# New orders for the attention stage of a parallel transformer block, and a weight split moved to GpSimd

## Chip, cores and metric

The kernel runs on one core of a Trainium2 chip. The metric is the device time in microseconds (us) of one execution. TensorE (PE, its weight loads PEld), VectorE (DVE), ScalarE (ACT), GpSimd (POOL) and the DMA queue of SyncE (SP) each work through their own instructions in program order; semaphores make one wait for another.

## What is computed

A row of 448 values for each of 2048 tokens is normalised, goes through multi-query attention (16 heads of 28, one shared key and value head) and, normalised again, through a channel MLP (448 to 1792 to 448, GELU). The sum of input, attention and MLP is the output, all in float32:

```python
def _A_ref(x, wq, wk, wv, wo):          # S=2048, D=448, H=16, Dh=28
    q = (x @ wq).reshape(B, S, H, Dh).transpose(0, 2, 1, 3)
    k, v = x @ wk, x @ wv
    scores = einsum("bhqd,bkd->bhqk", q, k) * (Dh ** -0.5)
    o = einsum("bhqk,bkd->bhqd", softmax(scores), v)
    return o.transpose(0, 2, 1, 3).reshape(B, S, H * Dh) @ wo
xn = layernorm(x)
return x + _A_ref(xn, wq, wk, wv, wo) + _B_ref(xn, w1, b1, w2, b2)   # _B_ref: layernorm, GELU MLP
```

## The kernel before, in words

The first part (to about 349 us of the span) normalises, makes queries, keys and values and runs the MLP. It is not changed. Its last steps already compute the scores of the first two key tiles of attention.

Attention is 16 units, `units`: four chunks of 512 query tokens times four groups of four heads. A unit meets 16 key tiles of 128 tokens. All of TensorE's results go to the eight banks of PSUM (each 128 partitions by 512 floats), which are handed out in a ring: `bank_number` takes the next one modulo 8 (L606), so that a user waits for whoever read the bank eight turns ago. The pieces of work are:

- `scores` (L612), one key tile: four banks, one for each head; 12 matmuls of 32x512 (L618), three terms of the split float32 product, the four heads side by side on four row strips of the array. Then ScalarE takes exponentials from the banks to a tile `p` in SBUF (L625). A digit after the `s` in the order says which neighbouring banks share an instruction: bit j joins bank j with bank j+1 (s5 = 0-1 and 2-3, s6 = 0 and 1-2-3, s2 = 0, 1-2, 3, s4 = 0, 1, 2-3, s1 = 0-1, 2, 3, s0 = four apart). Banks 7 and 0 are not neighbours, so a join across the ring's end falls away.
- `pv` (L735), the weighted sum of 1, 2 or 3 key tiles (P1, P2, P3): one bank; eight matmul instructions a key tile (L739), four heads on four column strips, in plain float32 and so in two passes. VectorE then adds the bank to a running sum `oc` (L731 the first, L733 the others) and so frees it. The weighted sums run two key tiles behind the scores.
- `m`, `find_max` (L540): one matmul against the first key tile (L523) for a bound on the next unit's scores, then four VectorE steps and a DMA (L524 to L531) that put the bound into that unit's queries. These queries come by four DMAs, issued at the start of the unit before (`load_unit`, L533, L538).
- `Q`, `out_tile` (L703): the output product of one tile of 128 tokens of the chunk before, 12 matmuls (L701) with the split output weights `woh`, `wol`, a VectorE add to the loaded row and a DMA out. `T` does the same ahead of time for the last chunk, `E` is the last weighted sum and the end of the kernel.
- After a unit's last weighted sum VectorE normalises (L714 to L722) in two parts, put in between the adds, and GpSimd makes the low half of the split result (L723).

Nothing but a table sets the order: `ORDERS` (L34) has one string for units 0 to 3, one for 4 to 14, one for 15. The loop at L836 goes through its words and calls these pieces, and each engine gets its instructions in that order. After the third word of unit 0 the loop also calls `split_out` (L681), which splits the output weights `wor` into a rounded high half and the rest. `wor` comes by four DMAs issued when attention begins (L678).

Of the kernel before, what the change touches and what calls it, by code (L numbers as in the profile page):

```python
# [14 lines left out]
ALU = mybir.AluOpType  # L15
# [15 lines left out]
MLP_ORDER = 1, 2, 3, 0  # L31
HD = D // 2
WEIGHTS = 7
ORDERS = ("s5 P1 s6 s6 P2 s6 s5 P2 s4 s1 m P2 s6 P1 s6 s5 P2 s6 s6 P2 s6 s5 P2 s6 s4 P2",  # L34
          "s5 P1 s6 s6 P2 s6 s5 P2 s6 s6 P2 s6 s5 P2 s2 s2 P2 s2 m Q s2 s6 P3 s6 s4 P2",
          "s5 P1 s6 s6 P2 s6 s5 P2 s6 s6 P2 s6 s5 P2 s2 s2 P2 s2 m Q s2 s6 P2 T T T E3")
FIRST_BANK = 0
LIMITS = 0.25, 2.0 ** 40

# [2 lines left out]
def block_kernel(ctx, tc, x, wq, wk, wv, wo, w1, b1, w2, b2, out):  # L42
    nc = tc.nc
    pe, act, dve, pool = nc.tensor, nc.scalar, nc.vector, nc.gpsimd
    ctx.enter_context(tc.manual_schedule())

    def f(t):
        return t.bitcast(F32)
# [418 lines left out]
    for c in range(NCH):  # L467
        if c + 1 < NCH:
            center, turn = norm_parts(c + 1, False)
        for i in range(4):  # L470
# [24 lines left out]
            if i in ((1, 3), (1, 2), (1, 3), (0, 2))[c]:  # L495
                n = 2 * c + (i - 1 if c == 1 else i // 2 if c == 3 else i // 3)
# [36 lines left out]
    def load_unit(u):  # L533
        c, g = units[u]
        qs = qss[u] = qst[u % 2]
        for j in range(4):
            rs = slice(DH * (4 * g + j), DH * (4 * g + j + 1))
            nc.sync.dma_start(f(qs[32 * j:32 * j + DH, :, :]), qd[rs, :, c * CW:(c + 1) * CW])  # L538
# [73 lines left out]
    def scores(u, kt, joined):  # L612
        at = [bank_number() for j in range(4)]
        keys = slice(kt * P, (kt + 1) * P)
        for n, (i, h) in enumerate(((0, 0), (0, 1), (1, 0))):
            for j in range(4):
                rs = slice(32 * j, 32 * j + 32)
                pe.matmul(bank(at[j]), ks[rs, i, keys], qss[u][rs, h, :], start=(n == 0), stop=(n == 2))  # L618
        p = early.pop(0) if early else att.tile([P, 4, CW], F32, name=f"p{next(turn_p) % WEIGHTS}", bufs=1)
        j = 0  # L620
        while j < 4:
            n = 1
            while j + n < 4 and joined >> (j + n - 1) & 1 and at[j + n] == at[j] + n:
                n += 1
            act.activation(p[:, j:j + n, :], banks[:, at[j]:at[j] + n, :], AF.Exp, scale=SCALE)  # L625
            j += n
        ps[u, kt] = p
# [43 lines left out]
    def weights_tile():  # L671
        t = xl_p.tile([P, 4, CW], F32R, name="xl").rearrange("p b n -> p (b n)")
        return t[:, 0:NG * D].rearrange("p (g d) -> p g d", g=NG)

    wor = f(weights_tile())
# [3 lines left out]
    woh, wol = weights_tile(), weights_tile()  # L679

    def split_out():  # L681
        dve.tensor_copy(woh, wor)
        dve.tensor_sub(wol, wor, f(woh))


    sums = keep.tile([P, NU, CW // 32], F32, name="sums")
# [3 lines left out]
    def load_rows_of(c):  # L690
        for k in range(CT):
            rows[c, k] = att.tile([P, D], F32, name="row", bufs=2 * CT)
            nc.sync.dma_start(rows[c, k], ad[:, CT * c + k, :])
# [55 lines left out]
    def last_burst(n, flag):  # L749
        u = NU - 1  # L750
        c, g = units[u]
        oc = pos.pop(u)
        tr, rb = (att.tile([P, CW], F32, name=name) for name in ("tr2", "tr"))
        rc = att.tile([P, CW // 32], F32, name="rc")
        halves = [(slice(256 * i, 256 * i + 256), slice(8 * i, 8 * i + 8)) for i in range(2)]
        sides = []
        for h, r in halves:
            po = score_bank()[:, 0:256]
            for k in range(NT - n, NT):
                for j in range(4):  # L760
                    pe.matmul(po[32 * j:32 * j + 32, :], vs[:, k, :], ps[u, k][:, j, h],
                              start=(k == NT - n), stop=(k == NT - 1))
            sides.append(po)
        ahead(CT - 1)
        for i, (h, r) in enumerate(halves):
            dve.tensor_add(oc[:, h], oc[:, h], sides[i])
            dve.transpose(tr[:, h], oc[:, h])
            if i == 1:
                copy = flag(blocks(tr)[:, :, 0])
            dve.reciprocal(rc[:, r], blocks(tr[:, h])[:, :, 0])  # L770
            dve.transpose(blocks(rb[:, h]), rc[:, r, None].to_broadcast([P, 8, 32]))
            dve.tensor_mul(oc[:, h], oc[:, h], rb[:, h])
            if i == 1:
                copy()
            for k in (2 * i, 2 * i + 1):
                pe.matmul(outs[k], oc[:, k * P:(k + 1) * P], wor[:, g, :], start=False, stop=True)  # L776
        for k in range(CT):
            a = rows[c, k]
            if k == 1:
                act.activation(tr[:, 0:D], outs[k], AF.Copy)  # L780
                pool.tensor_add(a, a, tr[:, 0:D])
            else:
                dve.tensor_add(a, a, outs[k])
            (nc.scalar if k % 2 else nc.sync).dma_start(ov[:, CT * c + k, :], a)
# [6 lines left out]
    def weighted(count):  # L791
        n = done[0]
        done[0] += count
        u, kt = divmod(n, NT)
        pv(u, kt, count)
        n += count - 1
        if n % NT == NT - 1:
            norm = norm_jobs(u, pos.pop(u))
            soon(n + 1, lambda: next(norm))
            soon(n + 3, lambda: next(norm))  # L800
        for m in sorted(at):
            if m <= n:
                for job in at.pop(m):
                    job()

    def token(kind, u):
        if kind == "m" and u + 1 < NU:
            find_max(u + 1)
        elif kind == "m":
            extremes(sums.rearrange("p u e -> p (u e)").bitcast(I32), worst)  # L810
        elif kind == "Q":
            c, k = units[u]
            out_tile(c - 1, k, range(NG))
        elif kind == "T":
            ahead(len(outs))
# [20 lines left out]
    for u in range(NU):  # L836
        if u + 1 < NU:
            load_unit(u + 1)
        if units[u][1] == 0 and u:
            load_rows_of(units[u][0] - 1)  # L840
        if u == NU - 2:
            load_rows_of(NCH - 1)
        for n, word in enumerate(ORDERS[(u >= NG) + (u == NU - 1)].split()):
            kind, times = word[0], int(word[1:] or 1)
            if kind == "s" and todo:
                scores(*todo.pop(0), times)
            elif kind == "P":
                weighted(times)
            elif kind == "E":
                last_burst(times, flag)  # L850
            else:
                token(kind, u)
            if (u, n) == (0, 2):
                split_out()
    outside = nc.values_load(count)
    with tc.If(outside > 0, preferred_fallthrough_block=True, label="outside"):
# [45 lines left out]
```

## Time and profile before

| | us |
|---|---|
| median of 3 runs (lowest, highest) | 894.08 (893.58, 894.96) |
| the profiled execution's own time | 893.52 |
| its span, from first to last instruction | 891.7 |
| TensorE busy in the span | 875.2 |
| ScalarE busy in the span | 650.1 |
| VectorE busy in the span | 360.7 |
| GpSimd busy in the span | 155.3 |
| attention after its first stretch, 366.70 to 877.60 | 510.90 |
| of that ScalarE busy | 474.35 |

A row of the timeline has the start, the time to the end of the last instruction, the engine, the line, the operation, what is written from what is read, shapes and count; in brackets the engine's idle time before it and what ended that. Matmuls overlap in the array, so the distance from one row's start to the next one's start, and not the row's length, is what a burst costs. In a row of groups the numbers behind the bar are busy us in total, mean ns of one, and idle us before them with what ended it.

### The profile page before, as it was taken

To read this page: it belongs to the slowest core of one execution; us is meant where nothing else is said; L and a number is where in the kernel's file an instruction comes from. 1 tells how busy PE (TensorE), PEld (TensorE's weight loads), DVE (VectorE), ACT (ScalarE), POOL (GpSimd) and SP (SyncE) were. 2 spreads that over 40 slices of the span, in tenths; PEclk is the share of its full clock that TensorE was granted. 3 is DMA by queue.
4 is the path that set the end of the run, shared out by engine and by line. 5 is a ranking of instruction groups with operands and counts; after the bars stand their busy time and mean duration, and the time that the engine had idled before them with its cause. 6 is when DMAs were issued, how large, how long until landed. Compare 5 with 4: busy or idle time off the path is not lost.

```text
span 891.7 us, 16976 instructions
## 1 busy us (share of the span) xinstructions
PE 875.2 (98%) x6997; PEld 529.5 (59%) x6997; DVE 360.7 (40%) x654; ACT 650.1 (73%) x890; POOL 155.3 (17%) x149
## 2 busy tenths in 40 slices
PE   9999999999999999899999999999999999999997
PEld 8877888888888886333434444444444444444444
DVE  7865454335345353342343234233233233333323
ACT  5765443333443436799999898898898899899891
POOL 7443243242234332000000000000000000000000
PEclk9999999999999999999999999999999999999999
DMA  9792112002001103000002101102101102102001
GB/s 301 215 288 81 42 63 83 1 1 83 21 21 51 44 11 91 9 22 22 9 16 64 33 1 33 33 2 74 32 1 33 33 1 74 33 1 73 12 1 54
DMA packets 28957, 46.02 MB, mean 52 GB/s; under 512 B 4542, under 2 KB 20492, under 8 KB 28876
## 3 DMA queue, kind: packets, MB, share of 16 engines
q1 hardware_dynamic: 27468, 44.32, 16.1%
q8 instruction: 56, 0.92, 0.4%
q10 hardware_dynamic: 1408, 0.57, 0.2%
q14 instruction: 25, 0.20, 0.1%
HBM read 28.22 MB, written 14.68 MB: 48 GB/s over the span
## 4 chain that ended last, share of the span: by engine, by line
PE 87%; ACT 7%; issue 2%; DVE 2%; DMA 1%; SPq 0%; DVEq 0%; ACTq 0%
PE banks L618 24%; PE banks L739 23%; PE banks L180 15%; PE banks L590 15%; ACT p L625 5%; PE banks L701 4%; PE banks L185 2%; PE banks L183 2%; PE banks L304 1%; PE banks L523 1%; DMA xl<-in_A_wo_dram 1%; DMA qd<-qe 0%; DVE w2l L382 0%; PE banks L776 0%; DMA rows<-in_A_x_dram 0%
## 5 line engine op out<-in xcount | busy, mean ns | idle before, releaser
L625 ACT ACTIVATE p<-banks 128x1024 f32<-128x1024 f32 (+2 forms) x623 | 484.8, 879 | 39.5 <-PE banks L618 36.4
L618 PE MATMUL banks<-xh,ks 32*128 32x512 f32 x3072 | 256.1, 424 | 6.4 <-DVE oc L733 4.3
L618 PEld LDWEIGHTS banks<-xh,ks 32*128 32x128 f32 x3072 | 145.0, 183 | 168.0 <-ACT p L625 142.7
L739 PE MATMUL banks<-p,vs 128*32 128x512 f32 x2008 | 243.4, 601 | 0.0
L733 DVE TENSOR_TENSOR oc<-oc,banks 128x512 f32<-128x512 f32 x115 | 78.9, 686 | 304.0 <-PE banks L739 245.9
L739 PEld LDWEIGHTS banks<-p,vs 128*32 128x32 f32 x2008 | 52.2, 109 | 120.9 <-issue 80.4
L564 ACT ACTIVATE hx<-banks,b1t 128x512 f32<-128x512 f32 x56 | 38.5, 688 | 110.7 <-PE banks L185 103.7
L572 POOL TENSOR_TENSOR hl<-hx,hh 128x512 fp32r<-128x512 f32 x56 | 76.8, 1371 | 182.3 <-DVE hh L571 176.9
L723 POOL TENSOR_TENSOR otl<-oc,oth 128x512 fp32r<-128x512 f32 x15 | 19.2, 1280 | 487.7 <-DVE oth L722 487.7
L566 DVE SCALAR_TENSOR_TENSOR hz<-hz,hx 128x512 f32<-128x512 f32 x56 | 44.3, 792 | 101.6 <-ACT hz L565 101.3
L590 PE MATMUL banks<-w2l,hh 128*128 128x448 f32 x220 | 81.0, 368 | 0.8 <-DVE w2l L382 0.7
L590 PE MATMUL banks<-w2h,hl 128*128 128x448 f32 x224 | 81.4, 366 | 0.0
L590 PE MATMUL banks<-w2h,hh 128*128 128x448 f32 x220 | 81.0, 368 | 0.1
L567 ACT ACTIVATE hz<-hz 128x512 f32<-128x512 f32 x56 | 35.4, 632 | 48.5 <-DVE hz L566 48.5
L180 PE MATMUL banks<-xl,w1h 128*128 128x512 f32 x168 | 65.7, 391 | 0.0
L180 PE MATMUL banks<-xh,w1l 128*128 128x512 f32 x168 | 65.6, 391 | 0.0
L180 PE MATMUL banks<-xh,w1h 128*128 128x512 f32 x168 | 65.5, 390 | 0.0
L568 DVE SCALAR_TENSOR_TENSOR hx<-hz,hx 128x512 f32<-128x512 f32 x56 | 39.1, 698 | 42.9 <-ACT hz L567 42.9
L590 PEld LDWEIGHTS banks<-w2l,hh 128*128 128x128 f32 x220 | 41.3, 188 | 7.1 <-DVE w2l L382 3.2
L590 PEld LDWEIGHTS banks<-w2h,hh 128*128 128x128 f32 x220 | 41.3, 188 | 6.0 <-issue 0.7
L590 PEld LDWEIGHTS banks<-w2h,hl 128*128 128x128 f32 x224 | 42.1, 188 | 3.3
L565 ACT ACTIVATE hz<-banks,b1s 128x512 f32<-128x512 f32 x56 | 38.2, 682 | 0.0
(156 smaller groups left out, 765.3 us busy)
## 6 DMA issues: line engine op xcount, KB each, us to landing
xh<-qd SPq DMA_DIRECT2D x64, 112.0 KB
qd<-qe SPq DMA_DIRECT2D x12, 512.0 KB
a<-in_A_x_dram SPq DMA_DIRECT2D x24, 224.0 KB
ad<-a SPq DMA_DIRECT2D x16, 224.0 KB
row<-ad SPq DMA_DIRECT2D x16, 224.0 KB
raw<-in_B_w_dram SPq DMA_DIRECT2D x7, 448.0 KB
out_dram<-row SPq DMA_DIRECT2D x14, 224.0 KB
ks<-qe SPq DMA_DIRECT2D x16, 112.0 KB
```

The lines of the kernel that those rows point to most:

```text
L180: pe.matmul(ps, w, v, start=(n == 0), stop=False)
L564: act.activation(hx, ph, AF.Identity, bias=b1t[:, ft:ft + 1])
L565: act.activation(hz, ph, AF.Square, bias=b1s[:, ft:ft + 1], scale=GELU[0] ** 0.5)
L566: dve.scalar_tensor_tensor(hz, hz, 1.0, hx, op0=ALU.add, op1=ALU.mult)
L568: dve.scalar_tensor_tensor(hx, hz, 1.0, hx, op0=ALU.add, op1=ALU.mult)
L572: pool.tensor_sub(hl, hx, f(hh))
L590: pe.matmul(m2[k], h[:, k * P:(k + 1) * P], w[:, ft, :], start=(ft == 0 and i == 0), stop=(ft == NF - 1 and i == 2))
L618: pe.matmul(bank(at[j]), ks[rs, i, keys], qss[u][rs, h, :], start=(n == 0), stop=(n == 2))
L625: act.activation(p[:, j:j + n, :], banks[:, at[j]:at[j] + n, :], AF.Exp, scale=SCALE)
L701: pe.matmul(po, ots[c, g][o][:, ts], w[:, g, :], start=(n == 1), stop=(stop and n == 3 * len(gs)))
L733: dve.tensor_add(pos[u], pos[u], po)
L739: pe.matmul(po[32 * j:32 * j + 32, :], vs[:, k, :], ps[u, k][:, j, :], start=(k == kt), stop=(k == kt + n - 1))
```

## The change

All three orders are new. In units 0 to 3 every key tile's scores are followed by one weighted sum. In units 4 to 15 this holds for eight tiles, then the work comes in longer bursts around `m` and `Q` as before. Which banks share an exponential follows the new places in the ring. `find_max` moves from behind seven score tiles to behind five in units 0 to 3. `split_out` is now done by GpSimd, and is called after the third word of unit 2.

```diff
-ORDERS = ("s5 P1 s6 s6 P2 s6 s5 P2 s4 s1 m P2 s6 P1 s6 s5 P2 s6 s6 P2 s6 s5 P2 s6 s4 P2",
-          "s5 P1 s6 s6 P2 s6 s5 P2 s6 s6 P2 s6 s5 P2 s2 s2 P2 s2 m Q s2 s6 P3 s6 s4 P2",
-          "s5 P1 s6 s6 P2 s6 s5 P2 s6 s6 P2 s6 s5 P2 s2 s2 P2 s2 m Q s2 s6 P2 T T T E3")
+ORDERS = ("s2 P1 s4 P1 s2 P1 s2 P1 s1 P1 m s2 P1 s4 P1 s2 P1 s2 P1 s2 P1 s4 P1 s4 P1 s4 P1 s2 P1 s2 P1 s2 P1",
+          "s2 P1 s2 P1 s2 P1 s2 P1 s2 P1 s4 P1 s4 P1 s0 P1 s6 P2 s4 s4 m Q s0 s1 P3 s6 s4 P2 s2 P1",
+          "s2 P1 s2 P1 s2 P1 s2 P1 s2 P1 s4 P1 s4 P1 s0 P1 s6 P2 s4 s4 m Q s0 s1 P3 s6 T T T E3")
...
     def split_out():
-        dve.tensor_copy(woh, wor)
-        dve.tensor_sub(wol, wor, f(woh))
+        pool.tensor_scalar(woh, wor, 1.0, 0.0, op0=ALU.mult, op1=ALU.add)
+        pool.tensor_sub(wol, wor, f(woh))
...
-            if (u, n) == (0, 2):
+            if (u, n) == (2, 2):
                 split_out()
```

On TensorE, in unit 1 (order 0), from its `find_max` (L523) on, this stood before (L618 scores, x12 is one key tile; L739 weighted sums, one row and x4 a key tile, each of the four run as two passes):

```order
 L523 MATMUL banks<-xh,kd 128x512
 L739 MATMUL banks<-p_3399,vs 32x512 x4
 L739 MATMUL banks<-p_3414,vs 32x512 x4
 L618 MATMUL banks<-xh,ks 128x512 x12
 L739 MATMUL banks<-p_3438,vs 32x512 x4
 L618 MATMUL banks<-xh,ks 128x512 x24
 L739 MATMUL banks<-p_3454,vs 32x512 x4
 L739 MATMUL banks<-p_3487,vs 32x512 x4
 L618 MATMUL banks<-xh,ks 128x512 x24
```

and this stands there now:

```order
 L523 MATMUL banks<-xh,kd 128x512
 L618 MATMUL banks<-xh,ks 128x512 x12
 L739 MATMUL banks<-p_3420,vs 32x512 x4
 L618 MATMUL banks<-xh,ks 128x512 x12
 L739 MATMUL banks<-p_3441,vs 32x512 x4
 L618 MATMUL banks<-xh,ks 128x512 x12
 L739 MATMUL banks<-p_3470,vs 32x512 x4
 L618 MATMUL banks<-xh,ks 128x512 x12
```

Two tiles' scores in a row, then two tiles' weighted sum in one bank, have become one and one; each weighted sum has its own bank and its own add. In unit 5 (order 1), ahead of its `find_max`, this stood on TensorE before:

```order
 L739 MATMUL banks<-p_4847,vs 32x512 x4
 L618 MATMUL banks<-xh,ks 128x512 x24
 L739 MATMUL banks<-p_4872,vs 32x512 x4
 L739 MATMUL banks<-p_4887,vs 32x512 x4
 L618 MATMUL banks<-xh,ks 128x512 x12
 L523 MATMUL banks<-xh,kd 128x512
```

and now:

```order
 L618 MATMUL banks<-xh,ks 128x512 x12
 L739 MATMUL banks<-p_4931,vs 32x512 x4
 L618 MATMUL banks<-xh,ks 128x512 x12
 L739 MATMUL banks<-p_4952,vs 32x512 x4
 L739 MATMUL banks<-p_4973,vs 32x512 x4
 L618 MATMUL banks<-xh,ks 128x512 x24
 L523 MATMUL banks<-xh,kd 128x512
```

Pairs have become singles up to the last two tiles, and ahead of L523 stands a pair where a single stood. Behind it, product, pair, P3, pair, P2 and a single follow as before.

On VectorE, where attention begins (L595 the MLP's last adds, L731 and L733 the first adds of unit 0, L682 and L683 the split, L524 on `find_max`):

```order
 L595 TENSOR_TENSOR a<-a,banks 128x448 x4
 L731 COPY oc<-banks 128x512
-L682 CAST xl<-xl 128x1792
-L683 TENSOR_TENSOR xl<-xl 128x1792
+L733 TENSOR_TENSOR oc<-oc,banks 128x512 x4
+L524 STREAM_TRANSPOSE tm<-banks 128x512
```

The two instructions of the split are gone from between the first add and the second.

On GpSimd the two instructions stand behind the low half (L723) of unit 0's result and ahead of that of unit 1's; the other fourteen follow.

## The prediction

> **What bounds the kernel now.** I read the page first, then the two stretches of TensorE's timeline below, then the exponentials by form and the first microseconds of attention. The page says how little room there seems to be on TensorE:
>
> ```profile
> PE 875.2 (98%) x6997; PEld 529.5 (59%) x6997; DVE 360.7 (40%) x654; ACT 650.1 (73%) x890; POOL 155.3 (17%) x149
> PE 87%; ACT 7%; issue 2%; DVE 2%; DMA 1%; SPq 0%; DVEq 0%; ACTq 0%
> ```
>
> TensorE is on the chain for 87% of the span. But a matmul's busy time overlaps the next one's, so waits inside a burst hide in the 98%. I therefore read the starts. Here is unit 1 of attention (order 0) from one `find_max` matmul (L523) to the next; L618 rows are scores (x12 is one key tile), L739 rows weighted sums (x8 is one key tile):
>
> ```profile
> 397.83 0.49 PE L523 MATMUL banks<-xh,kd 128*128 128x512 f32 x1
> 398.25 1.92 PE L739 MATMUL banks<-p,vs 128*32 128x512 f32 x16
> 400.11 0.96 PE L618 MATMUL banks<-xh,ks 32*128 32x512 f32 x12
> 401.00 1.07 PE L739 MATMUL banks<-p,vs 128*32 128x512 f32 x8
> 402.00 0.97 PE L618 MATMUL banks<-xh,ks 32*128 32x512 f32 x12
> 403.16 0.97 PE L618 MATMUL banks<-xh,ks 32*128 32x512 f32 x12 [0.19 <-ACT p L625]
> 404.06 1.92 PE L739 MATMUL banks<-p,vs 128*32 128x512 f32 x16
> 405.91 1.94 PE L618 MATMUL banks<-xh,ks 32*128 32x512 f32 x24
> 407.78 1.92 PE L739 MATMUL banks<-p,vs 128*32 128x512 f32 x16
> ...
> 417.28 0.97 PE L618 MATMUL banks<-xh,ks 32*128 32x512 f32 x12
> 418.18 1.06 PE L739 MATMUL banks<-p,vs 128*32 128x512 f32 x8
> 419.17 2.19 PE L618 MATMUL banks<-xh,ks 32*128 32x512 f32 x24
> ...
> 428.92 0.50 PE L523 MATMUL banks<-xh,kd 128*128 128x512 f32 x1
> ```
>
> From start to start: one key tile's scores alone take 0.89 (400.11 to 401.00), its weighted sum 1.00, so a single "s P1" takes 1.89 (again 417.28 to 419.17). A P2 takes 1.855 (404.06 to 405.91 to the next, and 398.25 to 400.11). The unit lasts 31.09: 0.42 for L523, two singles (3.78), seven P2 (12.99), and the rest, 13.90, is seven pairs of scores, 1.99 each. Two single score tiles would be 1.78. The pair loses time in its second half: at 403.16 TensorE has stood still because ScalarE had not yet given back the banks of the tile before. A pair takes four of the eight banks twice in a row, and the second four are only free when ScalarE is through.
>
> Is ScalarE itself the limit? Its exponentials in attention after the first stretch, by form, and two places where two of a kind follow each other:
>
> ```profile
> L625 ACT ACTIVATE p<-banks 128x1024 f32<-128x1024 f32 x191 | 189.6, 1042 | 0.1
> L625 ACT ACTIVATE p<-banks 128x512 f32<-128x512 f32 x322 | 183.0, 609 | 32.1 <-PE banks L618 29.1
> L625 ACT ACTIVATE p<-banks 128x1536 f32<-128x1536 f32 x97 | 141.3, 1457 | 0.0
> 483.97 1.09 ACT L625 ACTIVATE p<-banks 128x512 f32<-128x512 f32 x2
> 487.44 1.95 ACT L625 ACTIVATE p<-banks 128x1024 f32<-128x1024 f32 x2
> ```
>
> Alone, an exponential costs 0.61 for one bank and 1.04 for two; queued, the second starts before the first has ended: 1.09 - 0.61 = 0.48 from start to start for one bank, 1.95 - 1.04 = 0.91 for two. So each further instruction costs only about 2 x 0.48 - 0.91 = 0.05. A key tile in two pieces costs ScalarE about 1.82 (twice 0.91), in three 1.87, in four 1.92. Its idle time, 32 us, is nearly all waiting for scores. ScalarE is close behind TensorE, and the eight banks between them set the waits.
>
> The second thing to see is at the start of attention, first VectorE's rows and then TensorE's:
>
> ```profile
> 356.64 1.09 DVE L682 CAST xl<-xl 128x1792 fp32r<-128x1792 f32 x1 [4.94 <-DMA xl<-in_A_wo_dram]
> 357.86 2.02 DVE L683 TENSOR_TENSOR xl<-xl 128x1792 fp32r<-128x1792 f32 x1
> 359.81 0.68 DVE L733 TENSOR_TENSOR oc<-oc,banks 128x512 f32<-128x512 f32 x1
> ```
>
> ```profile
> 349.80 1.07 PE L739 MATMUL banks<-xl,vs 128*32 128x512 f32 x8
> ...
> 354.74 1.49 PE L618 MATMUL banks<-xh,ks 32*128 32x512 f32 x15
> 360.54 1.48 PE L618 MATMUL banks<-xh,ks 32*128 32x512 f32 x9 [4.31 <-DVE oc L733]
> 361.95 3.00 PE L739 MATMUL banks<-p,vs 128*32 128x512 f32 x16
> 364.88 1.91 PE L618 MATMUL banks<-xh,ks 32*128 32x512 f32 x24
> ```
>
> The split of the output weights (L682, L683) stands in VectorE's queue ahead of the second add, and waits for its DMA until 356.64. The add behind it gives its bank back only at 360.5, and TensorE stands.
>
> **Part 1: the split.** The scores from 354.74 to 361.95 took 7.21 where a pair takes 1.99: 5.2 lost. The P2 behind it took 2.93 (361.95 to 364.88) in place of 1.855: 1.1 more: after the pause TensorE ran slower, and the stretch has a granted clock (0.91, the third number from the end) below 1:
>
> ```profile
> 349.00:367.00 18.00, 13.66 (x125) 5.45 (x125) 5.62 (x6) 10.75 (x15) 0.00 (x0) 0.91 0.44 109
> ```
>
> Together 6.3 us, on TensorE's path and so on the end. With the split on GpSimd, the adds follow one another. What is late next there: `find_max` of unit 0, which now comes after five singles: 349.80 + 1.00 + 4 x 1.89 = 358.36. It needs the queries of unit 1, and this is the DMA traffic from 344 to 362 in 40 slices of 0.45 us:
>
> ```profile
> GB/s 0 0 0 0 0 0 0 139 354 16 0 215 363 370 355 267 131 283 247 175 163 231 183 175 200 160 223 187 228 164 32 9 9 0 0 0 0 0 0 0
> ```
>
> It ends at 344 + 33 x 0.45 = 358.9, so a wait of 0 to 0.5; I take 0.3. The start gives 6.0.
>
> What the split costs GpSimd, from the nearest rows:
>
> ```profile
> L369 POOL TENSOR_TENSOR w1l<-pair,w1h 128x672 fp32r<-128x672 f32 x4 | 6.6, 1642 | 7.8 <-ACT w1h L368 7.7
> L153 POOL TENSOR_SCALAR wah<-pair 128x384 fp32r<-128x384 f32 x2 | 1.0, 514 | 0.1
> ```
>
> 1792 columns are 2.7 times 672, so 4.4 for the subtraction; 4.7 times 384, so 2.4 for the copy, both at most, since a fixed cost is scaled with them: up to 7 us against VectorE's 3.1. Behind it in GpSimd's queue is only L723's low half, one per unit. Both are first read by the products of unit 4, some 31 x 2 us later, so I cost it at nothing; without that cover it would be 7 us once. The Trainium skill, GPSIMD Engine Reference, section Engine selection, advises VectorE for elementwise work, GpSimd being about twice as slow with two inputs: the rows agree on the ratio, and by that alone the move would cost 3 to 4 us. It does not count here, since nothing waits.
>
> **Part 2: the orders.** Singles first. Let a single's scores start at 0. Its third set starts about 0.59 (two thirds of 0.89) and ScalarE about 1.08, when a matmul of the set is through (0.49, as long as L523's): both are estimates. The first bank is back at 1.08 + 0.61 = 1.69, the middle two (s2) at 1.08 + 0.48 + 1.04 = 2.60, the last at 1.08 + 0.48 + 0.91 + 0.61 = 3.08. The next tile's scores, at 1.89, need as their fourth bank the first of these (1.69, in time); the next weighted sum, at 2.78, the second (2.60, in time); the scores at 3.78 the last two (3.08) and the first bank of the tile between (1.89 + 1.69 = 3.58). The slack is about 0.2 everywhere, and ScalarE's 1.87 a tile is below 1.89, so no backlog grows; tiles in four pieces (1.92) come singly. Hence singles at 1.89.
>
> An order-0 unit is then 16 x 1.89 + 0.42 = 30.66 against 31.09: 0.43 less. For order 1, these rows run from one L523 to the next, with the row tile's product (12 matmuls, L701) behind the first:
>
> ```profile
> 534.70 0.50 PE L523 MATMUL banks<-xh,kd 128*128 128x512 f32 x1
> ...
> 537.56 1.74 PE L618 MATMUL banks<-xh,ks 32*128 32x512 f32 x24
> 539.27 2.78 PE L739 MATMUL banks<-p,vs 128*32 128x512 f32 x24
> 541.99 1.91 PE L618 MATMUL banks<-xh,ks 32*128 32x512 f32 x24
> 543.82 1.92 PE L739 MATMUL banks<-p,vs 128*32 128x512 f32 x16
> ...
> 567.69 0.50 PE L523 MATMUL banks<-xh,kd 128*128 128x512 f32 x1
> ```
>
> Before: 32.99. Now: nine singles 17.01; "s6 P2" 0.89 + 1.855; three pairs, at 1.71 (537.56, after the product, as before), 1.83 (541.99, after P3) and, ahead of `m`, 1.83 as the nearest case in which ScalarE has caught up; `m` and product 2.86; P3 2.72; P2 1.855. Sum 32.57: 0.42 less. Twelve such units and four of order 0: 12 x 0.42 + 4 x 0.43 = 6.8.
>
> VectorE adds once per tile now, 16 times a unit against 8 or 9. At about 0.69 each it has room, but where its normalisation stands ahead of an add, a bank comes late. Before, this made scores wait so often (total us, times):
>
> ```profile
> PEld banks L618: 2.0, 11
> ```
>
> That is in the rows above once; I take off 0.8 for more of it, with 0 and 2 as ends. The orders give 6.0.
>
> The sum: 12.0 off the profiled execution's 893.52 (span 891.7), so 881.5; its median of three is 894.08, so 882.1.
>
> A round trip between the two kinds of matmul has a price in these rows: P2 minus P1 is 0.855, so 0.145 of a P1 is fixed, and two single tiles cost 0.07 more than the pair at 1.71: about 0.22. Order 0 had 9 bursts of weighted sums a unit and now has 16, order 1 had 8 and now has 12: 4 x 7 + 12 x 4 = 76 trips more, 16.7 us. The sum holds them, because singles were measured with them. The waits they replace are the rest: 6.8 + 16.7 = 23.5.
>
> **The rivals.** (a) The orders give nothing: the 172 singles (4 x 16 and 12 x 9) each wait 0.035 for a bank, since the slack of 0.2 is worked out and not seen. 894.08 - 6.0 = 888.1. For it: ScalarE has 1.87 of each 1.89. Against: in unit 1 both singles ran free of waits. (b) The start's gain does not come, another first wait taking its place, the queries' DMA above all: 888.1 too; only 0.5 us of late landing is in sight. (c) Slower: the trips are paid and the waits stay, at the first set of each single's scores, which waits for ScalarE's release. Then 894.08 - 6.0 + 16.7 = 904.8. It decides against the change as soon as less than 16.7 - 6.0 = 10.7 of the 23.5 us of waits goes. The Trainium skill, TensorEngine Tiling (Array Packing), section Key Properties, speaks for it: a change of tiling mode, not only of tile, drains TensorE. The trace agrees that it costs, with 0.22 a round trip; the page gives no figure, and by its rule alone every trip added is a loss. Against (c): the pairs' waits are seen to come from holding eight banks at once, and singles do not.
>
> **How the numbers follow.** The forecast has 0.73, (a) 0.15, (b) 0.06, (c) 0.06. Bounds: pairs all at 1.71, no VectorE wait and all 6.3 at the start give 12 x 0.24 + 0.8 + 0.3 = 4.0 more, 878.1; pairs at 1.99 (0.32 a unit) and 2 for VectorE give 5 less, 887.1, and (a) and (b) lie at 888.1. Range 878.5 to 888.5. About 0.2%, 1.8 us, is what a measurement of this kernel can tell from no change. Faster 0.93, same 0.02, slower 0.05.
>
> **What would show it.** Right: no gap over 1 us on TensorE between 350 and 366 us of the span; L523 to L523 near 30.7 and 32.6 to 32.7; single scores at 0.89 to 0.90 between L739 rows; some 170 more exponentials, and nearly no TensorE wait on ScalarE. Wrong: singles at 1.95 or more with waits for L625, a gap ahead of unit 0's L523, or a product (L701) of unit 4 that waits for GpSimd.

## The result, and the profile after

The changed kernel takes 889.31 us (median of 5 runs, 888.39 to 889.7) against 894.12 for the kernel before in the same runs: a ratio of 0.9942, interval 0.9928 to 0.9955. It is faster by 4.8 us where 12.0 were forecast, and lies just outside the range (878.5 to 888.5). The profiled execution took 888.39, its span is 886.6 against 891.7.

The page after:

```profile
PE 870.8 (98%) x6997; PEld 511.8 (58%) x6997; DVE 411.7 (46%) x727; ACT 654.2 (74%) x1063; POOL 160.7 (18%) x151
PE 91%; DVE 4%; ACT 2%; DMA 2%; issue 1%; SPq 1%; ACTq 0%; DVEq 0%
```

ScalarE's share of the chain fell from 7% to 2%, as the orders were to do. But VectorE now has 4% where it had 2%, and DMA 2% where it had 1%. TensorE's start of attention:

```profile
357.44 1.06 PE L739 MATMUL banks<-p,vs 128*32 128x512 f32 x8
360.15 0.47 PE L523 MATMUL banks<-xh,kd 128*128 128x512 f32 x1 [1.65 <-DMA xh<-qd]
```

The stop of 4.31 us is gone. `find_max` was worked out to start at 358.36, but waits for the queries until 360.15. Then unit 1, first TensorE, then VectorE, then GpSimd:

```profile
393.28 0.97 PE L618 MATMUL banks<-xh,ks 32*128 32x512 f32 x12
394.18 1.06 PE L739 MATMUL banks<-p,vs 128*32 128x512 f32 x8
395.18 0.49 PE L618 MATMUL banks<-xh,ks 32*128 32x512 f32 x2
398.56 0.96 PE L618 MATMUL banks<-xh,ks 32*128 32x512 f32 x10 [2.89 <-DVE oc L733]
399.46 1.06 PE L739 MATMUL banks<-p,vs 128*32 128x512 f32 x8
```

```profile
391.16 0.69 DVE L733 TENSOR_TENSOR oc<-oc,banks 128x512 f32<-128x512 f32 x1 [0.73 <-PE banks L739]
391.76 0.71 DVE L524 STREAM_TRANSPOSE tm<-banks 128x512 f32<-128x512 f32 x1
392.50 0.69 DVE L525 TENSOR_REDUCE mr<-tm 128x16 f32<-128x512 f32 x1
393.23 3.96 DVE L529 TENSOR_SCALAR mn<-mr 128x16 fp32r<-128x16 f32 x1
397.22 0.71 DVE L530 STREAM_TRANSPOSE tm<-mn 128x512 f32<-128x512 f32 x1
397.86 0.65 DVE L733 TENSOR_TENSOR oc<-oc,banks 128x512 f32<-128x512 f32 x1
```

```profile
391.37 1.70 POOL L682 TENSOR_SCALAR xl<-xl 128x1792 fp32r<-128x1792 f32 x1
393.15 4.00 POOL L683 TENSOR_TENSOR xl<-xl 128x1792 fp32r<-128x1792 f32 x1
```

L529 negates 16 numbers a partition. In every other unit it takes 0.17 us; here 3.96. It starts 0.08 behind GpSimd's subtraction and ends 0.04 behind it. Two adds wait behind it in VectorE's queue, their banks come late, and the scores at 395.18 take 4.28 in place of 0.90: 3.4 us. The split was called in unit 2, but GpSimd, which had nothing else to do, reached it in unit 1, at once behind unit 0's low half.

In the rest, singles run as worked out. Unit 5 (order 1), from one L523 to the next:

```profile
529.77 0.49 PE L523 MATMUL banks<-xh,kd 128*128 128x512 f32 x1
532.80 1.80 PE L618 MATMUL banks<-xh,ks 32*128 32x512 f32 x24
534.53 2.78 PE L739 MATMUL banks<-p,vs 128*32 128x512 f32 x24
537.24 1.90 PE L618 MATMUL banks<-xh,ks 32*128 32x512 f32 x24
539.07 1.93 PE L739 MATMUL banks<-p,vs 128*32 128x512 f32 x16
540.93 0.97 PE L618 MATMUL banks<-xh,ks 32*128 32x512 f32 x12
541.83 1.07 PE L739 MATMUL banks<-p,vs 128*32 128x512 f32 x8
542.82 0.97 PE L618 MATMUL banks<-xh,ks 32*128 32x512 f32 x12
...
557.97 0.97 PE L618 MATMUL banks<-xh,ks 32*128 32x512 f32 x12
558.87 1.92 PE L739 MATMUL banks<-p,vs 128*32 128x512 f32 x16
560.72 1.89 PE L618 MATMUL banks<-xh,ks 32*128 32x512 f32 x24
562.54 0.49 PE L523 MATMUL banks<-xh,kd 128*128 128x512 f32 x1
```

The unit lasts 32.77; 32.57 was forecast. Nine singles take 17.04 (540.93 to 557.97; forecast 17.01), the pairs 1.73, 1.83 and 1.82 (1.71, 1.83, 1.83), P3 2.71. Only `m` with the product differs: 3.03 (529.77 to 532.80), not 2.86. Why is in the weight loads. Before, and then after:

```profile
534.70 0.19 PEld L523 LDWEIGHTS banks<-xh,kd 128*128 128x128 f32 x1 [0.36 <-ACT p L625]
534.81 0.42 PEld L701 LDWEIGHTS banks<-xl,oth 128*128 128x128 f32 x2
```

```profile
529.76 0.19 PEld L523 LDWEIGHTS banks<-xh,kd 128*128 128x128 f32 x1 [0.36 <-ACT p L625]
530.14 0.30 PEld L701 LDWEIGHTS banks<-xl,oth 128*128 128x128 f32 x2 [0.19 <-ACT p L625]
```

With a pair ahead of `m` in place of a single, the product waits for ScalarE; its first weights load 0.38 behind L523's instead of 0.11. The same holds for all eleven units with a product: `m` and product take 3.01 to 3.12 now and took 2.86 or 2.87 before.

### The profile page after: what moved, and what is told of

It is laid out like the page before. It is cut to its first block, busy times and chain, and to the rows that moved or that the text cites. A ratio compares the mean times of both kernels' runs of the same rounds, so it can differ in the third digit from the quotient of the medians.

```text
span 886.6 us, 17299 instructions
## 1 busy us (share of the span) xinstructions
PE 870.8 (98%) x6997; PEld 511.8 (58%) x6997; DVE 411.7 (46%) x727; ACT 654.2 (74%) x1063; POOL 160.7 (18%) x151
## 4 chain that ended last, share of the span: by engine, by line
PE 91%; DVE 4%; ACT 2%; DMA 2%; issue 1%; SPq 1%; ACTq 0%; DVEq 0%
PE banks L739 27%; PE banks L618 25%; PE banks L590 15%; PE banks L180 14%; PE banks L701 4%; PE banks L185 2%; PE banks L183 2%; PE banks L304 1%; PE banks L523 1%; DMA xh<-qd 1%; DVE mn L529 0%; DMA qd<-qe 0%; ACT p L625 0%; DVE w2l L382 0%; PE banks L776 0%
## 5 line engine op out<-in xcount | busy, mean ns | idle before, releaser
L625 ACT ACTIVATE p<-banks 128x512 f32<-128x512 f32 (+2 forms) x796 | 488.8, 777 | 30.8 <-PE banks L618 30.5
L739 PE MATMUL banks<-p,vs 128*32 128x512 f32 x2008 | 257.7, 602 | 0.0
L618 PE MATMUL banks<-xh,ks 32*128 32x512 f32 x3072 | 246.6, 421 | 3.1 <-DVE oc L733 2.9
L618 PEld LDWEIGHTS banks<-xh,ks 32*128 32x128 f32 x3072 | 135.3, 183 | 193.4 <-issue 93.9
L733 DVE TENSOR_TENSOR oc<-oc,banks 128x512 f32<-128x512 f32 x190 | 130.5, 687 | 243.1 <-PE banks L739 228.2
L723 POOL TENSOR_TENSOR otl<-oc,oth 128x512 fp32r<-128x512 f32 x15 | 19.2, 1281 | 476.7 <-DVE oth L722 243.9
L739 PEld LDWEIGHTS banks<-p,vs 128*32 128x32 f32 x2008 | 44.7, 108 | 102.1 <-ACT p L625 54.3
```

The lines of the kernel that those rows point to most:

```text
L733: dve.tensor_add(pos[u], pos[u], po)
```

## Experiments

The theory after the result: the start's gain came in full and the orders gave about 4 us. What is missing was taken by VectorE's wait for GpSimd (3.4), by the late queries (1.7), and by product and small waits in order 1 (about 2). The rivals: the start's gain or the orders' gain is smaller than thought, and L529's 4 us is a coincidence. Each kernel ran beside the kernel before on the same chip, and the ratios below are to that.

**The two halves apart.** The first has the orders of before and the split as changed; the second the new orders and the split as before.

```diff
 # e1_only_split: the changed kernel with
-ORDERS = ("s2 P1 s4 P1 ...
+ORDERS = ("s5 P1 s6 s6 P2 ...
 # e2_only_orders: the kernel before with
-ORDERS = ("s5 P1 s6 s6 P2 ...
+ORDERS = ("s2 P1 s4 P1 ...
```

> The orders of before, with the split alone moved to GpSimd and to unit 2. Theory (the split's wait at the start is gone, worth 6.3 us; GpSimd's subtraction then holds up VectorE's L529 of unit 1 by some 2.1 us, of which 1.5 reaches TensorE, because a bank is given back late): 894.1 - 4.8 = 889.3. Rival 1 (no hold-up of VectorE by GpSimd in itself): 887.8. Rival 2 (the start's gain needs the new orders): about 894.

> The new orders, with the split on VectorE at the start as before. Theory (the trace after shows about 4 us from the orders, 0.3 a unit, and the start's wait of 6.3 us stays, which also hides the late queries): 894.1 - 4.0 = 890.1. Rival (the orders give the 6.0 of the forecast, and something else took it in the changed kernel): 888.1.

Only the split: 888.75, ratio 0.9935 (0.9921 to 0.9948). Only the orders: 890.74, ratio 0.9956 (0.9942 to 0.997). The second lies nearer to its theory (890.1) than to its rival (888.1). The first lies between its theory (889.3) and rival 1 (887.8), and by its ratio, which gives 888.3 at 894.1, nearer to the rival: the time does not decide it, and the trace does. With the orders of before, `find_max` of unit 1 stands elsewhere, and L529 meets only the end of the subtraction:

```profile
L529 DVE TENSOR_SCALAR mn<-mr x16: 174/174/2304, 315.6 to 829.6; 128x16 fp32r<-128x16 f32 x16
```

(least, median and greatest time in ns of its 16 instances): 2.1 us late, where 2.1 was worked out from GpSimd's rows. Of the 1.5 expected on TensorE 1.2 came: unit 1's L523 to unit 2's takes 32.34, and 31.11 in the unit before. The two halves alone save 5.7 and 3.7, and together only 4.8: each costs the other something, since the new order brings `find_max` earlier, ahead of its queries and under the whole subtraction. Nor are the 3.7 the orders alone, for the second run pays more at the start:

```profile
355.14 0.50 PE L618 MATMUL banks<-xh,ks 32*128 32x512 f32 x2
361.08 1.65 PE L618 MATMUL banks<-xh,ks 32*128 32x512 f32 x10 [5.45 <-DVE oc L733]
362.66 1.94 PE L739 MATMUL banks<-p,vs 128*32 128x512 f32 x8
364.52 1.65 PE L618 MATMUL banks<-xh,ks 32*128 32x512 f32 x12
```

TensorE stands for 5.45 us, and the weighted sum behind takes 1.86 (362.66 to 364.52) where 1.00 is usual.

**What makes L529 wait.** Four runs. First its result is written to every second float:

```diff
-mn = keep.tile([P, CW // 32], F32R, name="mn", bufs=2)
+mn = keep.tile([P, CW // 32, 2], F32R, name="mn", bufs=2)[:, :, 0]
```

> The changed kernel with one edit: L529's result is written to every second float. Theory (L529 waits because in its packed form it needs what GpSimd's subtraction holds; a strided result takes it out of that form): L529 of unit 1 back from 3.96 us to under 0.3, 3.4 us less, 889.3 - 3.4 = 885.9. Rival (whatever VectorE starts just then waits for GpSimd, or the wait is for something else): L529 stays at 3.96, 889.3.

It took 889.63, ratio 0.994 (0.9926 to 0.9954), the same as without the edit, and

```profile
L529 DVE TENSOR_SCALAR mn<-mr x16: 174/175/3957, 316.3 to 829.4; 128x16 fp32r<-128x16 f32 x16
```

So the theory was wrong about the packed form, or the rival right. The next run does the negation by another kind of instruction:

```diff
-dve.tensor_scalar(mn, mr, -1.0, 0.0, op0=ALU.mult, op1=ALU.add)
+dve.tensor_reduce(mn, mr[:, :, None], axis=AX.X, op=ALU.max, negate=True)
```

> The changed kernel with L529's negation done by a reduction over one element that negates, in place of multiplying by a number. Theory (it is the kind of the instruction that makes VectorE wait for GpSimd; a reduction is not of that kind, as L525 ran at 0.69 us beside GpSimd's copy): L529 of unit 1 under 0.4 us, 3.4 us less, 885.9. Rival (any VectorE instruction that starts during GpSimd's subtraction waits for it): L529 stays at 4 us, 889.3.

It took 884.61, ratio 0.9891 (0.9877 to 0.9905):

```profile
L529 DVE TENSOR_REDUCE mn<-mr x16: 169/170/171, 315.9 to 824.2; 128x16 fp32r<-128x16 f32 x16
393.16 4.04 POOL L683 TENSOR_TENSOR xl<-xl 128x1792 fp32r<-128x1792 f32 x1
393.23 0.17 DVE L529 TENSOR_REDUCE mn<-mr 128x16 fp32r<-128x16 f32 x1
393.43 0.71 DVE L530 STREAM_TRANSPOSE tm<-mn 128x512 f32<-128x512 f32 x1
```

The same 16 numbers, in the same place beside the same subtraction, no longer wait, and the transposition behind them runs beside it at its usual 0.71. It is the kind of instruction, not the moment. The Trainium skill, SBUF — State Buffer, section Who interferes with whom, says this: VectorE shares one pair of SBUF ports with GpSimd, a VectorE copy, cast or tensor_scalar in a two-port form needs it, whoever comes first has it for the whole instruction and the other stands still, and a reduction never needs it. These runs agree, with 3.96 beside 4.00 and 0.17. That the stride changed nothing agrees with the Trainium skill, VectorE: DVE Perf Modes, section What auto-detection actually checks, by which two ports are taken if both sides lie in SBUF and their outer sizes are even or equal (16 and 16 here); the step is no condition for 32-bit values.

Then the cost doubled, and the held time cut:

```diff
 # e5_split_twice
-if (u, n) == (2, 2):
+if (u, n) in ((2, 2), (3, 2)):
 # e6_split_in_four
-pool.tensor_scalar(woh, wor, 1.0, 0.0, op0=ALU.mult, op1=ALU.add)
-pool.tensor_sub(wol, wor, f(woh))
+for g in range(NG):
+    pool.tensor_scalar(woh[:, g], wor[:, g], 1.0, 0.0, op0=ALU.mult, op1=ALU.add)
+    pool.tensor_sub(wol[:, g], wor[:, g], f(woh[:, g]))
```

> The changed kernel with the split done once more in unit 3 (the same values again). Theory (GpSimd's subtraction stands ahead of find_max in time in each order-0 unit and holds up VectorE's L529): a second L529 of about 4 us, in unit 2, and 3.4 us more: 889.3 + 3.4 = 892.7. Rival (the hold-up in unit 1 was a coincidence of that unit): 889.3.

> The changed kernel with the split in four pieces of 448 columns, copy and subtraction in turn. Theory (VectorE waits for the one GpSimd instruction that runs, not for GpSimd to be idle): L529 of unit 1 at most 1.2 us, nearly no wait on TensorE, 889.3 - 3.3 = 886.0. Rival (GpSimd's next instruction is served before VectorE): L529 stays at 3 to 4 us, 889.3.

Twice: 894.69, ratio 1.0002 (0.9991 to 1.0012), 5.4 us more and not 3.4. Four pieces: 884.84, ratio 0.9895 (0.988 to 0.9909), with L529 at

```profile
L529 DVE TENSOR_SCALAR mn<-mr x16: 174/174/519, 315.5 to 823.8; 128x16 fp32r<-128x16 f32 x16
```

VectorE is served between GpSimd's pieces: L529 of unit 1 waits for the end of one copy of 0.57, and not for the subtraction behind it. The second split hits unit 2 (L529 3.78) as the first hit unit 1, and why it costs more than 3.4 is on TensorE there:

```profile
430.25 0.49 PE L618 MATMUL banks<-xh,ks 32*128 32x512 f32 x2
433.46 1.65 PE L618 MATMUL banks<-xh,ks 32*128 32x512 f32 x10 [2.72 <-DVE oc L733]
435.03 1.94 PE L739 MATMUL banks<-p,vs 128*32 128x512 f32 x8
436.90 1.65 PE L618 MATMUL banks<-xh,ks 32*128 32x512 f32 x12
438.48 1.06 PE L739 MATMUL banks<-p,vs 128*32 128x512 f32 x4
```

Behind the pause a weighted sum takes 1.87 and not 1.00, a tile's scores 1.58 and not 0.89: TensorE runs slower for some 5 us. The granted clock (third number from the end) says the same. Here are the stretches behind the pause, first behind the pause above, then behind unit 1's in the run with the strided result and in the changed kernel:

```profile
433.40:439.00 5.60, 5.54 (x34) 2.08 (x38) 1.38 (x3) 2.42 (x5) 0.00 (x0) 0.50 0.00 1
398.50:404.00 5.50, 5.43 (x42) 1.81 (x44) 1.39 (x3) 3.63 (x6) 0.00 (x0) 0.69 0.00 1
398.50:404.00 5.50, 5.44 (x58) 1.95 (x58) 2.07 (x4) 4.49 (x8) 0.00 (x0) 1.00 0.00 1
```

In these three a unit with the pause lasts 36.59, 35.69 and 34.19 from L523 to L523, where 30.8 is usual: the pause costs 3.4 us at the full clock and 4.9 or 5.8 with a slow stretch behind it. The twelve runs of this kernel scatter accordingly: four with a mean granted clock of 0.996 or more over the run took 891.55 to 893.38 us, eight with less 894.3 to 896.48. The profile of the changed kernel, at 0.999, is its fastest run; its other four, at 0.996 to 0.998, took 0.9 to 1.3 us more. So the hold-up being worth 4.2 to 4.7 us by these runs and 3.4 by that trace fits slow stretches in the other executions. Why one pause of nearly 3 us is followed by a slow stretch and another is not stays open.

**The late queries.** They are loaded behind the output weights on one queue; here ahead of them:

```diff
 load_unit(u + 1)
+if u == 0:
+    load_wo()          # the four loads of wor, before: ahead of the loop
```

> The changed kernel with the four loads of unit 1's queries issued ahead of the four loads of the output weights. Theory (unit 0's find_max waits 1.7 us for queries that stand behind the weights in the queue): no TensorE gap ahead of L523 in unit 0, 889.3 - 1.7 = 887.6. Rival (the wait is the latency of these loads, or another gap takes its place): 889.3.

It took 887.91, ratio 0.992 (0.9907 to 0.9934). `find_max` of unit 0 starts without a wait, near the 358.36 of the forecast:

```profile
358.72 0.49 PE L523 MATMUL banks<-xh,kd 128*128 128x512 f32 x1
```

In its trace the way from unit 1's L523 to unit 2's is 1.4 us longer than in the changed kernel's (389.56 to 425.20, against 390.96 to 425.15), with the slow pace seen above behind the pause; of its five runs four had a granted clock of 0.996, and the one at 0.999 took 886.39. The next run has both mends:

```diff
 # e10_loads_and_form: both edits
+if u == 0:
+    load_wo()
-dve.tensor_scalar(mn, mr, -1.0, 0.0, op0=ALU.mult, op1=ALU.add)
+dve.tensor_reduce(mn, mr[:, :, None], axis=AX.X, op=ALU.max, negate=True)
```

> The changed kernel with both the queries' loads ahead of the weights' and L529 as a reduction. Theory (the two waits are independent): 889.3 - 1.7 - 3.4 = 884.2. Rival (one takes the place of the other, or another first wait comes): 886 or more.

It took 883.27, ratio 0.9877 (0.9863 to 0.9891): 1.3 us below the reduction alone. The two waits are independent, and this kernel beats both others.

**The halves again, without the waits.** The mended kernel with the orders of before, and with the new order in units 0 to 3 alone:

```diff
 # e11_mended_old_orders: e10_loads_and_form with the three orders of before
 # e12_mended_new_order0: the same with the first of the three orders new
```

> The orders of before in the mended kernel (split on GpSimd in unit 2, queries loaded first, L529 as a reduction). It separates the two halves of the change where neither meets the other's waits. Theory (the start's wait is worth 6.3 us and the orders the 4.5 us that the traces show): 894.1 - 6.3 = 887.8, so 4.5 above the 883.3 of the mended kernel with the new orders. Rival 1 (the orders give the forecast's 6.0): 889.3. Rival 2 (they give 2.5 or less): 885.8 or less.

> The mended kernel with the new order in units 0 to 3 alone, the orders of before in units 4 to 15. Theory (the traces show 0.31 us less for each order-0 unit and 0.27 for each later one): 887.8 - 1.2 = 886.6. Rival (singles hold most of the gain, and only order 0 is all singles): 885.3 or less.

Orders of before: 887.55, ratio 0.9923 (0.9909 to 0.9936). New order 0 alone: 886.0, ratio 0.9905 (0.9889 to 0.992). Against 0.9877 for all new orders this gives, at 894.1 us, 6.9 for the start, 4.1 for the orders, of which 1.6 lie in units 0 to 3 (7 trips more each) and 2.5 in units 4 to 15. Each ratio's interval reaches 1.2 to 1.4 us to either side, and 886.0 lies between the theory (886.6) and the rival (885.3), so the times leave this split open. The traces settle it: from L523 to L523 units 0 to 3 take 31.11 with the old order and 30.78 with the new one (means of three), and later units 33.05 and 32.87 (means of ten, all orders old against all new). That is 0.33 in each of four units and 0.18 in each of twelve, 3.5 of the 4.1 between the traces: the rival that singles hold most of the gain, and so order 0, falls.

## Why the prediction was wrong, point by point

The sum had two terms of 6.0. By the ratios the change is 6.9 (start) + 4.1 (orders) - 4.6 (L529) - 1.3 (queries) = 5.1 us. The four are steps on one path from kernel to kernel, so they must add up to the change itself (4.8 by the medians, 5.2 by the ratio), and their sum proves none of them. By the traces they are 6.3, 4.1, 3.4 and 1.7.

1. **The start**: right in mechanism and size. 6.3 were worked out before taking off the late queries; 6.9 were measured by the runs, and 6.3 between the spans of the two traces (891.7 and 885.4).
2. **"so I cost it at nothing"**: this step failed, and the range with it. I asked who waits for GpSimd's result, and nobody does until unit 4. I did not ask what runs beside it: the split takes 5.7 us (1.70 + 4.00; 7 was the bound), and for the 4.0 of the subtraction L529 stands still, with two adds behind it and the banks that these free. Without this one wait the kernel takes 884.61, well inside the range. The contention could be read in the trace of before, in the MLP, where a VectorE instruction with two inputs in SBUF ran beside GpSimd's; its group, and its longest instance with GpSimd's row beside it:

```profile
L566 DVE SCALAR_TENSOR_TENSOR hz<-hz,hx x56: 677/693/1541, 67.3 to 340.7; 128x512 f32<-128x512 f32 x56
124.19 1.15 POOL L644 TENSOR_TENSOR a<-a,b2b 128x448 f32<-128x448 f32 x1
124.34 1.54 DVE L566 SCALAR_TENSOR_TENSOR hz<-hz,hx 128x512 f32<-128x512 f32 x1 [1.26 <-ACT hz L565]
```

   Of the 56, 14 took more than 0.75 us, and every one of these started while a GpSimd add or subtraction ran. I also took "called in unit 2" for a time; on an idle engine it is only a place in the queue.
3. **"a wait of 0 to 0.5; I take 0.3"**: mis-sized, 1.7 in the trace and 1.3 by the runs. The traffic had ended at 358.9 in the trace of before; `find_max` started at 360.15. In the changed kernel the same traffic ended about 0.9 us later (0.45 us slices, at 359.75), and `find_max` started 0.4 behind its end; the forecast let it start at the end.
4. **The orders**: right in mechanism, 4.1 and not 6.0. Units 0 to 3 gave nearly what was worked out (1.6 by the runs, 4 x 0.33 = 1.3 by the traces, against 1.7). In units 4 to 15 the failed term is "`m` and product 2.86": 3.03, because the product behind the pair waits for ScalarE, 1.9 us in the eleven units that have one. I carried over a row from a place where a single stood ahead. The 0.8 taken off for VectorE's late adds was more than was needed: what weight loads for scores waited for adds went from 2.1 us before to 2.4 in the mended kernel.
5. **The range** took its lower end from the best case of every term and its upper from "the orders give nothing". It held no case in which GpSimd costs VectorE something, the one resource that the moved instructions newly met.
6. **Rivals**: (a) and (c) fell: the orders gave 4.1, and singles did run at 1.89 with 76 trips more, so the trips were paid for out of the waits. (b) held in part, with the mechanism it named: the queries' DMA.

## What to carry to other kernels

Work moved to an idle engine is free only if that engine shares nothing with the others while it runs: look at what stands beside it, and cut long GpSimd instructions into pieces, or give VectorE beside them a kind of instruction that ran on here, such as the reduction. Place in a program is not a time: on an idle engine an instruction runs as soon as its inputs are there and the work ahead of it in the queue is done. A pause can cost more than its length when a slow stretch of TensorE follows. When a step is moved forward, every input of it must be checked for its landing, and a row for a composite step holds only behind the same neighbours.

## What the runs showed of the hardware

A VectorE tensor_scalar of 16 columns waited out a GpSimd subtraction of 4.00 us (3.96, and 2.30 when it met only the end), strided or not; as a reduction it took 0.17. After pauses of 2.7 to 5.5 us TensorE sometimes ran slower for some 5 us, at a granted clock down to 0.50, and after one of 2.9 us it did not.

ScalarE's exponentials have longer rows in the denser schedule; by form, over attention after its first stretch, and eight of a kind in a row:

```profile
L625 ACT ACTIVATE p<-banks 128x512 f32<-128x512 f32 x582 | 319.6, 659 | 29.7 <-PE banks L618 29.4
L625 ACT ACTIVATE p<-banks 128x1024 f32<-128x1024 f32 x180 | 195.1, 1084 | 0.0
632.24 4.03 ACT L625 ACTIVATE p<-banks 128x512 f32<-128x512 f32 x8 [0.89 <-PE banks L618]
```

659 and 1084 ns, where 609 and 1042 were before. But they do not cost more: the eight take (4.03 - 0.67) / 7 = 0.48 us from start to start, with 0.67 for the last row alone, and over the whole stretch the median distance behind a one-bank exponential is 0.48 and behind a two-bank one 0.90 to 0.91, before and after. Only the rows overlap more. As with the matmuls, the distance between starts is the price, and not the length of a row.
